# A spectral gate with a feed-forward layer on one Trainium2 core: the last six pairs of w1 columns in seven half-size products

## The chip, the core and the metric

The kernel runs on one core of a Trainium2 chip. A core has TensorE (matrix products, "PE" in the profile, its weight loads "PEld"), VectorE ("DVE"), ScalarE ("ACT"), GpSimd ("POOL") and SyncE ("SP", which here only issues transfers). Each engine works through its own queue in the order in which the kernel writes its instructions, and waits where data or a buffer is missing. SBUF is the working memory of 128 partitions, and PSUM is the small memory of eight banks into which TensorE writes. The metric is the device time of one execution in microseconds.

## What is computed

```python
x  = A_x                                   # [1, 2048, 1024]
xn = layernorm(x)                          # over the last axis
X  = rfft2(xn) * (w_r + 1j * w_i)          # filter, [2048, 513]
s  = irfft2(X)
h  = silu(xn @ w1)                         # w1: [1024, 3584]
g  = silu(h @ w2)                          # w2: [3584, 1024]
out = x + s * g
```

All large products are made to nearly float32 precision with float16 operands: each operand is split into a high and a low half, and three matmuls (high x high, high x low, low x high) stand for one.

## The kernel before

**Two stages.** The first stage is `xn @ w1`. w1 has 28 tiles of 128 columns, and the 2048 rows of xn stand in four groups of 512, c = 0 to 3. One block (`mm1(c, f)`, L413) is 24 matmuls of 512 columns: eight slices of the 1024-long sum times three. It ends in one PSUM bank of the pool `pf`, which has four. The function that it returns empties the bank one block later with a ScalarE activation (Silu, L429). There are 112 blocks. Two w1 tiles make a pair q (0 to 13), and two row groups make a half g (0 or 1). When the four blocks of a pair and a half are done, `hidden` (L435) forms sums and differences of the four results, splits them into halves (ScalarE L216, then VectorE L219), and stores them in DRAM. They are the left operands of the second stage.

**The second stage** is `h @ w2`, already in seven products of half size (Strassen's scheme), m = 0 to 6. `w2_gen` (L367) loads the blocks of w2, or sums of them prepared in DRAM, and splits them. `mm2` (L494) multiplies and `acc` (L515) adds up on VectorE. Of the seven weight operands, three are sums that `w2max_gen` (L327) makes on VectorE and stores while it looks for the largest value of w2. Two more are summed by accumulating transfers (`SUMMED`).

**Background work.** Layer norm and the Fourier work run in between. `ln_gen(c)` (L643) normalises group c: `stats` takes mean and variance, and for c = 2 and 3 (`TURNED`) `turned` (L614) normalises on ScalarE, splits, and lets transfers transpose the halves. `fd_gen(c)` (L743) is the transform along the columns, `f_gen` (L872) the transform along the rows and the filter in 16 units, and `i_gen(c)` (L1100) the inverse. `weights1` (L226) loads w1 tiles, takes their largest value for a scale, and splits them. `wmax_gen` (L839) takes the largest value of the filter in 18 tiles.

**The order of the work** is written out by hand at build time. After each block, `after` (L1268) writes the pending steps of earlier blocks (`settle`), and `work` (L1274) takes one step of the w1 or w2 queue, one step of the queue of maxima in three of four calls, and up to three steps of the background queue:

```python
clock["dve"] = max(clock["dve"], clock["pe"] - 1.0)
for _ in range(3):
    if clock["dve"] > clock["pe"] + LEAD or hold[0] or slot(bg) == PAUSE:
        break
```

The two clocks are the planner's own tally of what it has written for VectorE and TensorE (`meter`, L179). ScalarE, GpSimd and transfers have no clock. The loop over `order` (from L1320 on) writes all 112 blocks: groups 0 and 1 with six tiles first, then groups 2 and 3 with the same six, then the rest pair by pair. The queue of maxima starts at block 22, when layer norm is done. The background queue holds ln, the four `fd_gen`, the filter and the inverse, in this order.

Of the kernel before, what the change touches and what calls it, by code (L numbers as in the profile page):

```python
# [9 lines left out]
F16 = mybir.dt.float16  # L10
# [12 lines left out]
LEAD, PAUSE, LAST, EARLY = 1.0, -1, 6, 2  # L23
IORDER = (1, 3, 0, 2)
SUMMED = (4, 5)
# [7 lines left out]
W2_BLOCKS = (((0, 0), (1, 1)), ((1, 0), (1, 1)), ((0, 0), (0, 1)), ((0, 0),), ((1, 0), (0, 0)), ((0, 1), (1, 1)), ((1, 1),))  # L33
RH = math.sqrt(0.5)
# [3 lines left out]
def _halves(v, scale):  # L38
    v = v * scale
    hi = v.astype(np.float16)  # L40
    return hi, (v - hi.astype(np.float64)).astype(np.float16)

# [54 lines left out]
def spectral_ffn(ctx, tc, x, w_r, w_i, w1, w2, ca, kc, ci, tw, pm, out):  # L97
# [11 lines left out]
    fp = ctx.enter_context(tc.tile_pool(name="fp", bufs=1))  # L109
    hstack = ExitStack()  # L110
# [9 lines left out]
    ws = {m: [dp.tile([128, 512], F32, name=f"ws{m}_{q}") for q in range(NP)] for m in range(3)}  # L120
# [9 lines left out]
    xsv = cp.tile([128, 3, 4, 4, 2], F32, name="xsv")  # L130
    e_w = small("e_w")
# [78 lines left out]
    e1, m1, r1, rs, s1 = (small(k, NFT) for k in ("e1", "m1", "r1", "rs1", "s1"))  # L210
    ep, hs = small("ep", NP), small("hs", NP)
    w2m = small("w2m", NFT)
# [8 lines left out]
    def column_sums(name, m, n):  # L221
        ps = pf.tile([128, 512], F32, name=name, tag="ff")
        nc.tensor.matmul(ps[:, 0:n], ones, m, start=True, stop=True)
        return ps[:, 0:n]

    def weights1():  # L226

        raw = {}

        def load(i):
            raw[i] = fp.tile([128, 8, 128], F32, name=f"w1r{i}", tag="w1", bufs=7)
            nc.sync.dma_start(raw[i], w1v[:, :, i * 128:(i + 1) * 128])
# [4 lines left out]
        def scales(i, k):  # L241
            sl = slice(i, i + k)
            ps = column_sums(f"s1_{i}", m1[:, sl], k)
            nc.vector.tensor_single_scalar(e1[:, sl].bitcast(I32), ps.bitcast(I32), 0x7F800000, op=OP.bitwise_and)
            nc.vector.tensor_single_scalar(e1[:, sl], e1[:, sl], 2.0**-100, op=OP.max)
            nc.vector.reciprocal(r1[:, sl], e1[:, sl])
            nc.vector.tensor_single_scalar(rs[:, sl], r1[:, sl], 2.0**14, op=OP.mult)  # L247
            nc.vector.tensor_single_scalar(s1[:, sl], e1[:, sl], 2.0**-24, op=OP.mult)
            if (i + k) % 2 == 0:
                p = (i + k) // 2 - 1  # L250
                nc.vector.tensor_tensor(ep[:, p:p + 1], e1[:, 2 * p:2 * p + 1], e1[:, 2 * p + 1:2 * p + 2], op=OP.max)
                nc.vector.tensor_tensor(hs[:, p:p + 1], r1[:, 2 * p:2 * p + 1], r1[:, 2 * p + 1:2 * p + 2], op=OP.min)
                nc.vector.tensor_single_scalar(hs[:, p:p + 1], hs[:, p:p + 1], 2.0**7, op=OP.mult)

        new = {}

        def split(i):
            new[i] = fp.tile([128, 2, 8, 128], F16, name=f"w1_{i}", tag="w1", bufs=7)
            high(new[i][:, 0], raw[i], rs[:, i:i + 1])

        def rest(i):
            w1t[i] = w = new.pop(i)
            low(w[:, 1], raw.pop(i), rs[:, i:i + 1], w[:, 0])
# [8 lines left out]
        scales(0, 2)  # L272
# [9 lines left out]
        scales(2, 2)  # L282
# [5 lines left out]
        yield 2  # L288
        def ahead(i):

            if i < NFT and i not in raw and i - len(used1) <= 4:
                load(i)
                load(i + 1)

        last = None
        for i in range(4, NFT, 2):
# [6 lines left out]
            maxi(i)  # L303
            if last is not None:
                rest(last)
            yield 0
            maxi(i + 1)
            yield 0
            ahead(i + 2)
# [3 lines left out]
            scales(i, 2)  # L313
            yield 0.8
            split(i)
            ahead(i + 2)
            yield 0.2
            rest(i)
            split(i + 1)
# [3 lines left out]
        rest(last)  # L323

    used1 = set()

    def w2max_gen():  # L327

        ap = A["p"]
        junk = ap.tile([128, 1024], F16, name="junk", tag="junk", bufs=1)  # L330
        tiles = {}
        for i in range(NFT + 3):
            if i < NFT:
                tiles[i] = ap.tile([128, 1024], F32, name=f"w2m{i}", tag="x", bufs=4)
                nc.sync.dma_start(tiles[i], w2[i * 128:(i + 1) * 128, :])
            if 3 <= i <= NFT + 2:
                def both(m, x0, x1, op):
                    d = ap.tile([128, 512], F32, name=f"wd{m}_{i}", tag="wd", bufs=3)
                    nc.vector.tensor_tensor(d, x0, x1, op=op)
                    defer(1, lambda q=(i - 3) // 2: stores[0].dma_start(ws[m][q], d))  # L340

                t_ = tiles.pop(i - 3)
                if i % 2:
                    both(0, t_[:, 0:512], tiles[i - 2][:, 512:1024], OP.subtract)
                both(1 + i % 2, t_[:, 0:512], t_[:, 512:1024], OP.add)
                nc.scalar.activation(junk, t_, AF.Abs, accum_out=w2m[:, i - 3:i - 2])
# [6 lines left out]
    def w2_scales():  # L353
# [7 lines left out]
        nc.vector.tensor_scalar(c2, e2, ee, 2.0**-20, op0=OP.mult, op1=OP.mult)  # L361
# [4 lines left out]

    def w2_gen():  # L367

        todo = [(m, q) for m in range(7) for q in range(NP)]
        raw = {}  # L370
# [23 lines left out]
        for n in range(4):  # L394
            load(n)
# [1056 lines left out]
```

## Time and profile before

| | us |
|---|---|
| median of two runs | 1293.58 |
| the runs | 1291.99 and 1295.17 |
| span of the profiled execution | 1291.9 |
| TensorE busy in it | 1264.8 |
| VectorE busy in it | 958.6 |
| ScalarE busy in it | 463.9 |
| GpSimd busy in it | 242.3 |

The profiled execution's own time is its span. A row of the groups reads: line of the kernel, engine, operation, output <- inputs, partitions x elements, count, then busy us and mean ns of one, then the idle time of the engine just before these instructions and what ended most of it. In the order of time a row reads: start us, duration us, engine, line, operation, and in brackets the idle time before it and what ended it. The row of a wait reads: engine, operation and line that waited, what it waited for, us in all, times, longest. The row of a transfer reads: output <- input, queue, count, KB of one, median us from issue to landing. "issue" is time for which the profile shows no cause.

### The profile page before, as it was taken

What the parts mean: (1) busy time and instruction counts of PE and PEld (TensorE: products, weight loads), DVE (VectorE), ACT (ScalarE), POOL (GpSimd) and SP (SyncE); (2) the same over time, 40 slices, a digit from 0 to 9 for tenths busy, and PEclk for the clock granted to TensorE, in tenths of its full rate; (3) what the DMA queues carried; (4) which work ended last, traced back from release to release, by engine and by line L of the source; (5) the groups of instructions that cost most, each with busy time, mean ns of one, the idle gap of its engine ahead of it and who ended that gap; (6) DMA issues with size and microseconds to landing.
All of it is one profiled execution on the core that took longest, in us unless ns stands there. A gap on an engine that the chain in (4) does not pass through costs nothing.

```text
span 1291.9 us, 18825 instructions
## 1 busy us (share of the span) xinstructions
PE 1264.8 (98%) x6991; PEld 656.7 (51%) x6991; DVE 958.6 (74%) x1964; ACT 463.9 (36%) x572; POOL 242.3 (19%) x389
## 2 busy tenths in 40 slices
PE   8999999999999999999999999999979999999997
PEld 5544445444544454445455555554445555656444
DVE  6688898899879898867679798993165565867544
ACT  4864343343545565534242311220131321333111
POOL 1231222223233443241221010104110100000000
PEclk9998999999999999999999999999989999999999
DMA  7576476555766896579889999984996799675995
GB/s 232 132 188 178 123 227 191 164 149 181 230 194 236 278 296 205 190 230 269 179 252 259 270 278 199 336 213 146 305 259 229 218 323 339 241 285 167 313 360 187
DMA packets 174955, 298.84 MB, mean 231 GB/s; under 512 B 38928, under 2 KB 91920, under 8 KB 174224
## 3 DMA queue, kind: packets, MB, share of 16 engines
q1 hardware_dynamic: 132464, 163.34, 42.5%
q0 software_dynamic: 26560, 82.86, 21.3%
q10 hardware_dynamic: 15840, 51.45, 11.3%
q8 instruction: 55, 0.90, 0.3%
q14 instruction: 36, 0.29, 0.1%
HBM read 189.06 MB, written 104.33 MB: 227 GB/s over the span
## 4 chain that ended last, share of the span: by engine, by line
PE 82%; DMA 8%; DVE 5%; ACT 2%; issue 2%; POOL 1%; SPq 0%; ACTq 0%; DVEq 0%; POOLq 0%
PE pa L420 39%; PE pb L498 10%; PE pb L499 10%; PE pb L500 10%; PE iu L1117 3%; PE id L1146 3%; DMA jr<-ws 2%; DMA hd_one<-hoone 2%; PE fx L902 1%; DMA zt<-zd 1%; ACT xp L657 1%; DMA jr<-in_B_w_dram 1%; DVE w L219 1%; DMA ht<-hd_sum 1%; PE fx L904 1%
## 5 line engine op out<-in xcount | busy, mean ns | idle before, releaser
L420 PE MATMUL pa<-xnT,w 128*128 128x512 f16 x2688 | 587.7, 380 | 5.6 <-DMA xnT<-xs 3.2
L420 PEld LDWEIGHTS <-w 128*128 128x128 f16 x2688 | 263.2, 98 | 319.0 <-issue 8.3
L498 PE MATMUL pb<-w,ht 128*128 128x512 f16 (+1 forms) x798 | 299.5, 375 | 0.2 <-DMA ht<-hd_sum_d 0.2
L499 PE MATMUL pb<-w,ht 128*128 128x512 f16 (+1 forms) x798 | 299.5, 375 | 0.0
L500 PE MATMUL pb<-w,ht 128*128 128x512 f16 (+1 forms) x798 | 299.5, 375 | 0.0
L429 ACT ACTIVATE h<-pa,s 128x512 f32<-128x512 f32 x112 | 75.8, 680 | 142.5 <-PE pa L420 135.7
L500 PEld LDWEIGHTS <-ht 128*128 128x128 f16 x798 | 78.1, 98 | 91.1
L498 PEld LDWEIGHTS <-ht 128*128 128x128 f16 x798 | 78.2, 98 | 88.5 <-DMA ht<-hd_sum_d 0.7
L499 PEld LDWEIGHTS <-ht 128*128 128x128 f16 x798 | 78.1, 98 | 87.8
L216 ACT ACTIVATE w<-jr,sc 128x512 f16<-128x512 f32 x98 | 67.7, 713 | 85.3 <-DMA jr<-in_B_w_dram 39.8
L219 DVE SCALAR_TENSOR_TENSOR w<-jr,sc,w 128x512 f16<-128x512 f32 x98 | 72.1, 748 | 25.9 <-ACT w L216 25.8
L219 DVE SCALAR_TENSOR_TENSOR hoone<-h,hs,hoone 128x2048 f16<-128x2048 f32 x28 | 65.8, 2348 | 19.6 <-ACT hoone L216 19.6
L452 POOL DMA_DIRECT2D hd_sum<-hosum x52 | 38.0, 767 | 209.8 <-DVE hosum L219 101.7
L216 ACT ACTIVATE hoone<-h,hs 128x2048 f16<-128x2048 f32 x28 | 55.9, 1997 | 40.3 <-DMA hd_one<-hoone 27.9
L216 ACT ACTIVATE hosum<-hr,hs 128x1536 f16<-128x1536 f32 x28 | 44.1, 1574 | 59.4 <-DVE hr L459 32.1
L452 POOL DMA_DIRECT2D hd_one<-hoone x52 | 45.5, 875 | 86.5 <-DVE hoone L219 52.5
L380 POOL DMA_DIRECT2D jr<-in_B_w_dram x28 | 24.6, 966 | 165.0 <-DMA jr<-in_B_w_dram 129.6
L458 DVE TENSOR_TENSOR hr<-h 128x1024 f32<-128x1024 f32 x28 | 34.2, 1223 | 28.0 <-ACT h L429 27.8
L1117 PE MATMUL iu<-kk,zt 128*128 128x256 f16 x384 | 45.3, 280 | 8.7 <-issue 8.7
L219 DVE SCALAR_TENSOR_TENSOR hosum<-hr,hs,hosum 128x1536 f16<-128x1536 f32 x28 | 50.8, 1814 | 1.9 <-ACT hosum L216 1.9
L216 ACT ACTIVATE w<-w1r,rs 128x1024 f16<-128x1024 f32 x28 | 32.0, 1146 | 49.6 <-DVE rs L247 20.2
L579 ACT ACTIVATE pl<-pl,c 128x512 f32<-128x512 f32 (+1 forms) x26 | 16.9, 682 | 89.5 <-DVE pl L558 45.9
(195 smaller groups left out, 1686.0 us busy)
## 6 DMA issues: line engine op xcount, KB each, us to landing
w1r<-in_B_w_dram SPq DMA_DIRECT2D x28, 512.0 KB, 6.2
w2m<-in_B_w_dram SPq DMA_DIRECT2D x28, 512.0 KB, 5.0
ht<-hd_dif ACTq DMA_DIRECT2D x32, 448.0 KB, 7.9
jr<-in_B_w_dram SPq DMA_DIRECT2D x56, 256.0 KB, 7.3
ht<-hd_sum ACTq DMA_DIRECT2D x32, 448.0 KB, 6.2
ht<-hd_one ACTq DMA_DIRECT2D x32, 448.0 KB, 5.2
hd_sum<-hosum POOLq DMA_DIRECT2D x52, 256.0 KB, 3.4
hd_one<-hoone POOLq DMA_DIRECT2D x52, 256.0 KB, 5.1
```

The costliest lines, as they stand in the source:

```text
L216: nc.scalar.activation(hi, raw, AF.Copy, scale=scale)
L219: nc.vector.scalar_tensor_tensor(lo, raw, scale, hi, op0=OP.mult, op1=OP.subtract)
L380: nc.gpsimd.dma_start(raw[n], w2_block(*todo[n], 1), accum_op=OP.add)
L420: nc.tensor.matmul(ps, w[:, wh, d], xt[:, xh, d], start=(n == 0), stop=(n == 23))
L429: nc.scalar.activation(hq[:, 2 * (c % 2) + f % 2], ps, AF.Silu, scale=s1[:, f:f + 1])
L452: defer(1, lambda k=k, m=m: stores[0].dma_start(hd[m, g][:, :, q].rearrange("f p h s -> f p (h s)"), o[:, k].rearrange("f p h s -> f p (h ...
L458: tt(sums[:, 0:2], hq[:, 0::2], hq[:, 1::2], op=OP.subtract)
L498: nc.tensor.matmul(ps, hh[:, 0], w[:, 0], start=first, stop=False)
L499: nc.tensor.matmul(ps, hh[:, 0], w[:, 1], start=False, stop=False)
L500: nc.tensor.matmul(ps, hh[:, 1], w[:, 0], start=False, stop=last)
L1117: nc.tensor.matmul(ps[:, q], lhs, rhs, start=(n == 0 and r == 0), stop=(n == 2 and r == 1))
L1146: nc.tensor.matmul(o, us[g][:, uh, 2 * p + r], C["ci"][:, ch, g, r], start=(n == 0 and r == 0), stop=(n == 2 and r == 1))
```

## The change

**w1.** The first 16 tiles are multiplied as before (64 blocks). The last six pairs are multiplied in seven half-size products each, per half g of the rows: the 1024-long sum is cut in two, the pair into its two tiles, the half into its two groups. `product(q, g, name)` is 12 matmuls. The products M1, M6, M7 and M4 add up in one PSUM bank, M5 and M3 go on in a second, M2 has a bank of its own, and ScalarE copies the first bank's partial sum out between the products:

```diff
+SLOTS = (("M1", 0), ("M6", 2), ("M5", 3), ("M7", 4), ("M2", 5), ("M4", 6), ("M3", 8))
+    def product(q, g, name):
+        a_, b_, s_ = W[q]
+        x0, x1, t_ = xnT[2 * g], xnT[2 * g + 1], T[g]
...
+        if name == "M1":
+            ae = pt.tile([128, 2, 512], F32, name=f"ae{q}_{g}", tag="ft")
+            units[q, g] = [ae[:, 0], ae[:, 1], None]
+        if name == "M2":
+            units[q, g][2] = pf.tile([128, 512], F32, name=f"pc{q}_{g}", tag="ff")
+        a, e, f = units[q, g]
+        ps = {"M2": f, "M3": e, "M5": e}.get(name, a)
+        for d in range(4):
+            for n, (wh, xh) in enumerate(((0, 0), (0, 1), (1, 0))):
+                nc.tensor.matmul(ps, lhs(d, wh), rhs(d, xh), ...)
...
+            if name == "M1":
+                act(hq[:, 2], a, AF.Copy)
+            elif name == "M6":
+                act(hq[:, 0], a, AF.Copy)
+            elif name == "M7":
+                act(hq[:, 1], a, AF.Copy)
+                tt(hq[:, 1], hq[:, 1], e, op=OP.add)
+                return lambda: (act(hq[:, 1], hq[:, 1], AF.Silu, scale=sc), None)[1]
+            elif name == "M4":
+                act(hq[:, 3], a, AF.Silu, scale=sc)
+            elif name == "M2":
+                tt(hq[:, 2], hq[:, 2], f, op=OP.add)
...
+            elif name == "M3":
+                tt(hq[:, 0], hq[:, 0], e, op=OP.add)
```

A unit is one (q, g); its products take places 7n + the offset in `SLOTS`, so that neighbouring units overlap by one product. The activation waits a stage after each add, and `hidden` follows as before.

**Operands.** `t_gen(g)` makes the sums of x that four of the products need, on VectorE and ScalarE, in the background queue after the first two `fd_gen`. `weights1` makes, for each of the last pairs, the split first tile, half of the second, and the split sums:

```diff
+    def t_gen(g):
...
+        for d in range(4):
+            b = view(R2[0], at * KB, [128, 4, 512], F32)
+            tt(b[:, 0:2], x1[:, 0, d::4], x1[:, 1, d::4], op=OP.add)
+            tt(b[:, 2:4], x0[:, 0, d::4], x0[:, 1, d::4], op=OP.add)
+            tt(b[:, 0], b[:, 2], b[:, 0], op=OP.subtract)
...
+            nc.scalar.activation(t_[:, d, :, 0], b, AF.Copy)
+            tt(t_[:, d, :, 1], b, t_[:, d, :, 0], op=OP.subtract)
+        for q in range(NPL, NP):
+            while not built[0]:
+                yield 0
+            r = view(R2[0], 64 * KB, [128, 2, 8, 128], F32)
...
+            high(a[:, 0], r[:, 0], sc)
+            low(a[:, 1], r[:, 0], sc, a[:, 0])
...
+            tt(r1[1], r1[0], r1[1], op=OP.add)
+            tt(r1[0], r0[0], r1[0], op=OP.subtract)
+            tt(r0[0], r1[1], r0[0], op=OP.subtract)
+            tt(r0[1], r0[1], r0[0], op=OP.subtract)
+            high(s_[:, 0, 0:8], rf[:, 0:8], sc)
```

`built` is true once the sums of x are done, and the first product comes only then.

**Memory.** xn, the sums of x and the weights stand in three fixed regions (`X1`, `R2`, `R3`), of which later tiles are views. `R2` opens only when the tiles of the first stage's pool are given back: `narrow` sets `hold_x`, which stops new loads in the queue of maxima, waits until the loaded tiles are used, and closes the pool. `hold_x` falls when the loop over the 64 blocks is done.

**Order.** The queue of maxima now takes w2 first (five steps for each two tiles), then the filter. What is left of it when the last pair starts is written out at once:

```diff
-LEAD, PAUSE, LAST, EARLY = 1.0, -1, 6, 2
+LEAD, PAUSE, EARLY = 2.5, -1, 2
+    for n, (_, u, name) in enumerate(plan):
...
+        if not w2j and (w1j.done and not xq or q == NP - 1):
+            finish(wq, w1j)
+            while xq:
+                slot(xq)
+            w2_scales()
+            w2j = add(wq, w2_gen())
+        ev = product(q, g, name)
```

The transforms of groups 2 and 3, and the whole filter, come in the second stage, and in the inverse some pauses go.

**Who does what.** The statistics of groups 2 and 3, and most maxima of w1, move to ScalarE:

```diff
+            if c in TURNED:
...
+                nc.scalar.activation(junk, xt, AF.Copy, accum_out=v[:, 0:1])
+                nc.gpsimd.tensor_single_scalar(v[:, 0:1], v[:, 0:1], -1.0 / D, op=OP.mult)
+                nc.scalar.activation(junk, xt, AF.Square, bias=v[:, 0:1], accum_out=v[:, 3:4])
...
+    def magnitude(raw, out):
+        junk = pf.tile([128, 512], F32, name="junk", tag="ff")
+        for k in range(2):
+            nc.scalar.activation(junk, raw[:, 512 * k:512 * k + 512], AF.Abs, accum_out=out[:, k:k + 1])
```

`magnitude` takes the sum of absolute values in place of the largest one. Two of the three sums of w2 that VectorE made are now made by accumulating transfers (`SUMMED = (1, 2, 4, 5)`). The column transform does two row tiles in one instruction, and in the filter a reordering moves from the butterflies to the split that follows them, so that both take fewer VectorE instructions. A pair of w1 tiles shares one scale.

673 lines of the change are left out of this document (443 added, 230 removed).

## The prediction

> **What bounds the kernel now.** I read the page first: engine sums, the TensorE clock by slices, the chain that ended last.
>
> ```profile
> span 1291.9 us, 18825 instructions
> PE 1264.8 (98%) x6991; PEld 656.7 (51%) x6991; DVE 958.6 (74%) x1964; ACT 463.9 (36%) x572; POOL 242.3 (19%) x389
> PEclk9998999999999999999999999999989999999999
> PE 82%; DMA 8%; DVE 5%; ACT 2%; issue 2%; POOL 1%; SPq 0%; ACTq 0%; DVEq 0%; POOLq 0%
> ```
>
> TensorE is busy 1264.8 of 1291.9 us, at full clock in nearly every slice, and is 82% of the chain. So the time is TensorE's work plus its few waits, and a change pays only if TensorE is still fed. Next I read the groups of instructions and busy times by stretch (after the colon of each stretch: its length, then PE, PEld, DVE, ACT, POOL busy, granted clock, DMA share, GB/s).
>
> ```profile
> L420 PE MATMUL pa<-xnT,w 128*128 128x512 f16 x2688 | 587.7, 380 | 5.6 <-DMA xnT<-xs 3.2 <-DVE xnT L674 1.7 <-ACT w L216 0.7
> 0.00:646.00 646.00, 635.28 (x3350) 312.61 (x3351) 531.27 (x1048) 308.09 (x346) 187.47 (x286) 0.99 0.68 204
> 646.00:1292.00 646.00, 629.52 (x3643) 344.14 (x3641) 427.36 (x916) 155.85 (x226) 54.79 (x103) 0.99 0.83 259
> 576.00:878.00 302.00, 300.90 (x1773) 156.93 (x1771) 253.83 (x489) 88.25 (x118) 40.34 (x64) 1.00 0.90 249
> ```
>
> The first product, 2688 matmuls at L420, fills the first 646 us and waits 5.6 us in all. VectorE is at 82% there (531 of 646), 66% in the second half, 84% in the stretch where the filter runs (576 to 878). None of that stops TensorE. What makes this work is slack: a block of 24 matmuls ends in one ScalarE activation, and four PSUM buffers let it come up to three blocks late. I therefore look at where the change spends that slack.
>
> **What it saves.** Blocks run back to back like this:
>
> ```profile
> 60.97 41.60 PE L420 MATMUL pa<-xnT,w 128*128 128x512 f16 x192
> 106.34 0.44 PE L420 MATMUL pa<-xnT,w 128*128 128x512 f16 x1 [2.43 <-DMA xnT<-xs]
> ```
>
> 192 matmuls in 41.60 us, the last one's run-out taken off, is 0.216 us each and 5.18 us a block. Seven products of 12 matmuls replace four blocks of 24, so 84 stand for 96. Six pairs times two groups are 12 units: 144 matmuls, **31.1 us** less. Other TensorE work only moves: two of four column transforms and all filter matmuls go to the second half. TensorE there has the same total, so I count the move at nothing; its cover is VectorE's free time, and the third rival prices its loss.
>
> **Layer norm on ScalarE, the start.** For column groups 2 and 3 the statistics go from VectorE to two ScalarE passes a tile. The planner hands out up to three background steps a block, while its VectorE clock is no more than LEAD ahead of TensorE's. A step that costs VectorE nothing always passes, so the steps of groups 2 and 3, spread now over blocks 4 to 11, all come out behind blocks 4 and 5. ScalarE, in order, then has them ahead of those blocks' own activations. Its present order:
>
> ```profile
> 51.64 0.69 ACT L429 ACTIVATE h<-pa,s 128x512 f32<-128x512 f32 x1
> 58.54 0.67 ACT L429 ACTIVATE h<-pa,s 128x512 f32<-128x512 f32 x1
> 65.39 0.67 ACT L429 ACTIVATE h<-pa,s 128x512 f32<-128x512 f32 x1
> 65.95 1.14 ACT L216 ACTIVATE w<-w1r,rs 128x1024 f16<-128x1024 f32 x1
> 71.42 1.15 ACT L216 ACTIVATE w<-w1r,rs 128x1024 f16<-128x1024 f32 x1 [4.33 <-DVE w L219]
> ```
> ```profile
> L657 ACT ACTIVATE xp<-x,v 128x1024 f32<-128x1024 f32 x8 | 17.3, 2163 | 0.0
> L635 ACT ACTIVATE xs<-xp 128x1024 f16<-128x1024 f32 x8 | 8.5, 1057 | 0.3
> L346 ACT ACTIVATE junk<-w2m 128x1024 f16<-128x1024 f32 x28 | 29.3, 1045 | 0.0
> L346 ACT ACTIVATION_READ_ACCUMULATOR junk<-w2m 128x1 f32 x28 | 5.3, 190 | 0.0
> ```
>
> These are the activations of blocks 3, 4 and 5, then the splits of the fifth and sixth w1 tiles. Normalising and splitting two tiles is 2 x (2.16 + 1.06) = 6.4 us. A statistics pass with its sum is 1.05 + 0.19 (the row nearest in form), so 4.9 us for two tiles. The activation of block 3 slides by 4.9 to 56.6. Ahead of block 4's then stand one w1 maximum (two 512-wide passes by the 0.69 row with their sums, 1.7), 6.4, 4.9 and 6.4: it starts at 56.6 + 0.7 + 19.4 = 76.7 instead of 58.5. Ahead of block 5's stand 4.9 + 6.4 + 4.9 + 6.4 = 22.6: it starts at 100.0. The fifth tile's split comes after that. With 1.14 and VectorE's low half (1.28, below) the tile is there at about 103, and block 8, which multiplies by it, began at 60.97 + 2 x 5.18 = 71.3. That is 32 us late, less the transposes' wait at 106 that falls away, plus slow clock:
>
> ```profile
> 104.00:108.00 4.00, 0.93 (x3) 0.31 (x4) 3.90 (x14) 3.89 (x4) 0.00 (x0) 0.81 0.91 186
> 108.00:112.00 4.00, 4.00 (x11) 1.44 (x10) 4.00 (x17) 0.00 (x0) 1.91 (x3) 0.50 0.38 116
> 112.00:116.00 4.00, 4.00 (x17) 1.63 (x15) 3.90 (x7) 0.45 (x1) 2.22 (x4) 0.83 0.67 196
> ```
>
> Here a wait of 3.1 us (4.00 - 0.93) was followed by 4 us at half clock and 4 at 0.83: 2.7 us lost beside the wait. Two new waits cost 5, the old one gives back 6. I take **+30**. Bounds: 15, if the new ScalarE work alone counts and fills the 4.3 us gap of the last row (8 tiles x 2.5 = 20, less that), and 45, if the loads for group 3, which now queue on SP behind all transposes of group 2, hold it as well.
>
> [...]
>
> **The hand-over to the seven products.** Its sums of x are the last background work before it. Prices:
>
> ```profile
> L219 DVE SCALAR_TENSOR_TENSOR hoone<-h,hs,hoone 128x2048 f16<-128x2048 f32 x28 | 65.8, 2348 | 19.6 <-ACT hoone L216 19.6
> L219 DVE SCALAR_TENSOR_TENSOR hosum<-hr,hs,hosum 128x1536 f16<-128x1536 f32 x28 | 50.8, 1814 | 1.9 <-ACT hosum L216 1.9
> L219 DVE SCALAR_TENSOR_TENSOR w<-w1r,rs,w 128x1024 f16<-128x1024 f32 x28 | 35.8, 1278 | 2.4 <-ACT w L216 2.4
> L458 DVE TENSOR_TENSOR hr<-h 128x1024 f32<-128x1024 f32 x28 | 34.2, 1223 | 28.0 <-ACT h L429 27.8
> L459 DVE TENSOR_TENSOR hr<-h 128x512 f32<-128x512 f32 x28 | 19.2, 686 | 0.0
> L239 DVE TENSOR_REDUCE m<-w1r 128x1 f32<-128x1024 f32 x28 | 33.9, 1214 | 5.5 <-DMA w1r<-in_B_w_dram 5.5
> L850 DVE TENSOR_REDUCE mw<-wm 128x1 f32<-128x912 f32 x18 | 19.7, 1096 | 0.0
> w1r<-in_B_w_dram SPq DMA_DIRECT2D x28, 512.0 KB, 6.2
> wm<-in_A_w_r_dram SPq DMA_DIRECT2D x9, 456.0 KB, 3.9
> wm<-in_A_w_i_dram SPq DMA_DIRECT2D x9, 456.0 KB, 3.7
> ```
>
> Eight rounds of 2 x 1.22 + 4 x 0.69 + 2.35 are 60 us. Beside them VectorE has per block a quarter of the hidden tiles' work (1.22 + 0.69 + 1.81 + 1.22 + 2.35 = 7.3) and some 0.35 of w1, 2.2 of 5.18 us, so the sums need about 20 blocks. They begin when the two transforms are done and the held queue of w2 maxima has drained. That queue starts at block 22, moves one step in three of four blocks and needs five steps for each of the three pairs that it holds by then: 15 steps, block 42 to 44 of 64. So the sums end with the last block. Only then may the first pair be loaded, into a place that the sums used. Two loads (6.2 each, overlapped, some 8), a maximum (1.2), a scale (1), high and low (1.14 + 1.28) are 12.6, less the 5.2 of the last block; M6 then waits some 3.5 more for the sums of the weights. **+11**; nothing if the sums end ten blocks earlier, 20 if VectorE runs behind.
>
> **In the products.** Five results of a unit share one bank: ScalarE must copy the partial sum before the next product adds, with one product (2.6 us) between. I take **+4**: 36 copies hidden cost 0, exposed 36 x 0.69 = 25; ScalarE is 48% busy in the first stage, so nearer the low end. VectorE's added work (60 for x, 36 adds of 0.69, four adds and one and a half lows more a pair) is some 113 us. It gives up 12 maxima of w1, 28 sums of w2 and eight tiles' statistics, 14.6 + 19.2 + 12 (the statistics as two 512-wide passes each, by L459): some 1026 us in all beside 1261 of time, so by its total it holds nothing up.
>
> **The burst before the last pair.** Maxima of w2 and of the filter advance one step in three of four products and stand still from the hold to the hand-over. 70 products give 52 steps; eleven of 14 pairs of w2 tiles are left at five steps each, so all 18 filter tiles remain, and the code drains them at once when the last pair starts. VectorE then takes 18 x 1.10 = 19.7 us without anything between, or, with three buffers of 3.8 to land and 1.1 to read, 18 x 1.63 + 3.8 = 33. Behind it in VectorE's queue is the low half of the hidden tile two units back, whose buffer M1's copy needs; M6 adds to what that copy reads. So TensorE gets two products (5.2 us), then waits: 19.7 + 2.4 + 0.7 - 5.2 = 17.6 up to 31. **+26**, nearer the loads' bound, slow clock within.
>
> **The second half.** More background work falls into it: two transforms and the first filter units. Its cover is the 34% of VectorE that is free there (646 - 427 = 219 us). The wait of TensorE in it today,
>
> ```profile
> PE iu L1117 <- issue: 8.7, 1, 8.7
> ```
>
> may come or go. Taken at **0**, between -9 and the +25 of the third rival.
>
> Sum on the profiled 1291.9: -31 + 30 + 11 + 4 + 26 = +40, **1332**; the median of the runs shown is 1.7 above the span, so **1334**.
>
> **Rivals.** *TensorE stays fed* (faster): ScalarE has 52% free in stage one, the pairs come in time, the drain hides behind PSUM buffers. For it: TensorE waits for ScalarE 0.7 us in all today. Against: those buffers do not cover a chain within one bank, nor 20 us of one queue. Time 1293.6 - 31 = 1262, or 1257 without the wait at 106; it decides if the new waits together stay under 5 us. Chance 0.18. *Half of it* (the same): the start or the drain is absorbed, not both: 1334 - 28 = 1306, or 1280 with the hand-over too. 0.2. *The late stage binds*: column transforms, filter and inverse in one half put VectorE, at 84% in 576 to 878 over 302 us, on the same filter in some 225 us, with DMA already 0.90; or every copy in the bank is exposed. 20 to 25 more: 1357. 0.1. The forecast has the remaining 0.52. That nothing is saved cannot be: the count of matmuls is fixed.
>
> **The numbers.** Two per cent, about what a measurement here can tell from no change, is 1267.7 and 1319.5. The forecast's own range is 1312 to 1352, from the bounds of the two largest terms half used up. The whole range, 1270 to 1362, leaves out most of the first rival and the worst of the third. Faster is the first rival, 0.18; within 2% the second and the low edge of the forecast, 0.25; slower 0.57.
>
> **What would show it.** TensorE idle 66 to 105 us with ScalarE solid in norms; a gap of some 10 us where the first block of 12 starts; a gap of about 25 before the last pair with 18 reductions in a row on VectorE; 2544 matmuls in place of 2688. If ScalarE's activations of blocks 4 and 5 start within 15 us of their blocks' ends, the first term is wrong; if the filter's reductions lie spread, the fourth is.

## The result, and the profile after

The changed kernel takes 1467.92 us (two runs, 1467.06 and 1468.78) against 1293.58: 1.135 times as long, with a 95% interval of 1.131 to 1.140. The prediction was 1334, with a range of 1270 to 1362. It was right that the kernel gets slower; the time lies 106 us above the top of the range.

The page of the changed kernel, in the lines that were shown of before:

```profile
span 1465.3 us, 18532 instructions
PE 1263.1 (86%) x6851; PEld 653.4 (45%) x6851; DVE 1002.4 (68%) x1696; ACT 570.6 (39%) x828; POOL 279.6 (19%) x417
PEclk9958999999979999985989999999898899989999
PE 25%; DMA 14%; DVE 9%; issue 2%; ACT 1%; POOL 1%; SPq 1%; ACTq 0%; DVEq 0%; POOLq 0%
```

TensorE is busy as long as before (1263.1 against 1264.8) with 140 fewer instructions. The chain that ended last is followed back only to about 686 us here, so its shares add up to 53% of the span; TensorE is 25 of these 53, where it was 82 of 100. The clock digits (TensorE's granted clock in tenths of full speed, in 40 slices) show where the time went: slices 3 and 4 (the start), 12 (the hand-over), 18 and 19 (before the last pair), and single ones in the second half. Cut at the first matmul of the second product, after and then before:

```profile
0.00:727.50 727.50, 599.33 (x2904) 281.21 (x2905) 492.66 (x650) 375.54 (x511) 173.46 (x276) 0.93 0.52 156
727.50:1465.30 737.80, 663.80 (x3949) 372.16 (x3947) 509.77 (x1047) 195.07 (x317) 106.09 (x141) 0.95 0.85 255
```
```profile
0.00:644.70 644.70, 633.98 (x3344) 312.02 (x3345) 531.27 (x1048) 308.09 (x346) 187.47 (x286) 0.99 0.68 203
644.70:1291.90 647.20, 630.82 (x3649) 344.73 (x3647) 427.36 (x916) 155.85 (x226) 54.79 (x103) 0.99 0.83 259
```

Length less PE busy is TensorE's idle time. In the first stage it goes from 10.7 to 128.2 us (+117.5), in the second from 16.4 to 74.0 (+57.6). So the whole loss, 173.4 in the spans, is 175.1 of idle time less 1.7 of busy time. Busy time falls by 34.7 in the first stage and rises by 33.0 in the second. The work that moved is smaller than that: half of the column transforms' 23.55 us and 8.28 us of the filter stood in the first stage before, 20.1 in all. So the second stage is busy 12.9 us longer than the moved work explains, and the first stage falls by 34.7 where the move and the 31.1 us saved would make 51.2. Together that is 29.4 us: nearly all that the fewer matmuls save goes in slower matmuls, at a granted clock of 0.93 and 0.95 (0.99 before).

What TensorE waited for, the largest lines of the view of waits:

```profile
PE ae L605 <- ACT h L617: 43.3, 6, 35.9
PE pa L565 <- ACT w L264: 35.8, 2, 35.3
PE iu L1377 <- DVE xn L1367: 31.4, 3, 12.6
PE fx L1124 <- DMA xn<-vd: 14.6, 3, 11.9
PE ae L605 <- ACT h L625: 12.6, 5, 9.5
PE s L279 <- DVE m L392: 10.8, 3, 8.2
PE fa L944 <- DMA r<-in_B_w_dram: 10.4, 1, 10.4
PE ae L605 <- ACT h L619: 8.2, 12, 0.7
```

L565 is a block of the first product as before, L605 one of the half-size products, fa, fx and iu are matmuls of the transform, the filter and the inverse. The names xn, r and w are now those of the three fixed regions, whatever stands in them.

**The start** went as the prediction says. ScalarE in the order of time, and the stretch of TensorE (of after, then of before):

```profile
55.00 0.71 ACT L575 ACTIVATE h<-pa,ep 128x512 f32<-128x512 f32 x1
...
74.91 0.67 ACT L575 ACTIVATE h<-pa,ep 128x512 f32<-128x512 f32 x1
82.36 1.06 ACT L854 ACTIVATE junk<-x 128x1024 f16<-128x1024 f32 x1 [6.77 <-DMA x<-in_A_x_dram]
...
106.07 0.67 ACT L575 ACTIVATE h<-pa,ep 128x512 f32<-128x512 f32 x1
106.64 1.14 ACT L264 ACTIVATE w<-w,rs 128x1024 f16<-128x1024 f32 x1
```
```profile
66.00:113.00 47.00, 8.40 (x53) 4.04 (x52) 11.90 (x16) 33.40 (x36) 7.26 (x24) 0.61 0.46 109
```
```profile
66.00:113.00 47.00, 43.83 (x208) 19.83 (x207) 40.45 (x61) 29.66 (x25) 12.38 (x15) 0.93 0.78 189
```

L575 are the activations of blocks 3, 4 and 5; between them stand two groups of statistics and norms. In 47 us TensorE does 53 instructions where it did 208.

**Before the last pair**, TensorE and then VectorE:

```profile
648.06 5.27 PE L605 MATMUL ae<-xn,w 128*128 128x512 f16 x12 [9.53 <-ACT h L625]
689.18 7.78 PE L605 MATMUL ae<-r,w 128*128 128x512 f16 x24 [35.86 <-ACT h L617]
```
```profile
647.59 1.09 DVE L1072 TENSOR_REDUCE mw<-xn 128x1 f32<-128x912 f32 x1
653.33 1.10 DVE L1072 TENSOR_REDUCE mw<-r 128x1 f32<-128x912 f32 x1 [4.64 <-DMA r<-in_A_w_i_dram]
...
682.25 1.10 DVE L1072 TENSOR_REDUCE mw<-xn 128x1 f32<-128x912 f32 x1
686.10 2.34 DVE L267 SCALAR_TENSOR_TENSOR hoone<-h,hs,hoone 128x2048 f16<-128x2048 f32 x1
```

The 18 reductions are in a row, most of them waiting for a load; behind them comes the low half of the hidden tile (hoone), and behind that the copy (L617) for which TensorE waits.

### The profile page after: what moved, and what is told of

It reads as the page before. It is cut to its first block, busy times and chain, and to the rows that moved or that the text cites. A ratio compares the mean times of both kernels' runs of the same rounds, so it can differ in the third digit from the quotient of the medians.

```text
span 1465.3 us, 18532 instructions
## 1 busy us (share of the span) xinstructions
PE 1263.1 (86%) x6851; PEld 653.4 (45%) x6851; DVE 1002.4 (68%) x1696; ACT 570.6 (39%) x828; POOL 279.6 (19%) x417
## 4 chain that ended last, share of the span: by engine, by line
PE 25%; DMA 14%; DVE 9%; issue 2%; ACT 1%; POOL 1%; SPq 1%; ACTq 0%; DVEq 0%; POOLq 0%
PE pb L700 6%; PE pb L701 6%; PE pb L702 6%; PE iu L1377 3%; DMA r<-in_B_w_dram 3%; DMA xn<-vd 2%; DMA zd<-xn 2%; PE id L1406 2%; PE ae L605 2%; DMA xn<-zd 2%; DMA fs<-gd 1%; DVE r L267 1%; DMA pd<-c 1%; PE fx L1124 1%; DMA xn<-in_A_w_i_dram 1%
## 5 line engine op out<-in xcount | busy, mean ns | idle before, releaser
L565 PE MATMUL pa<-xn,w 128*128 128x512 f16 x1536 | 336.6, 381 | 41.6 <-ACT w L264 35.8
L700 PE MATMUL pb<-r,w 128*128 128x512 f16 (+1 forms) x798 | 299.8, 376 | 0.0
L701 PE MATMUL pb<-r,w 128*128 128x512 f16 (+1 forms) x798 | 299.6, 375 | 0.0
L702 PE MATMUL pb<-r,w 128*128 128x512 f16 (+1 forms) x798 | 299.5, 375 | 0.0
L565 PEld LDWEIGHTS <-w 128*128 128x128 f16 x1536 | 150.3, 98 | 224.4 <-ACT w L264 36.3
L605 PEld LDWEIGHTS <-w 128*128 128x128 f16 x1008 | 100.5, 100 | 199.3 <-issue 82.8
L605 PE MATMUL ae<-r,w 128*128 128x512 f16 x576 | 135.2, 389 | 55.2 <-ACT h L617 43.3
L702 PEld LDWEIGHTS <-w 128*128 128x128 f16 x798 | 78.1, 98 | 91.4 <-issue 0.5
L700 PEld LDWEIGHTS <-w 128*128 128x128 f16 x798 | 78.3, 98 | 87.2 <-issue 0.2
L701 PEld LDWEIGHTS <-w 128*128 128x128 f16 x798 | 78.2, 98 | 87.1
L264 ACT ACTIVATE r<-r,sc 128x512 f16<-128x512 f32 x88 | 61.6, 716 | 130.2 <-DMA r<-in_B_w_dram 108.5
L267 DVE SCALAR_TENSOR_TENSOR r<-r,sc 128x512 f16<-128x512 f32 x88 | 65.0, 746 | 40.7 <-ACT r L264 40.7
L605 PE MATMUL ae<-xn,w 128*128 128x512 f16 x288 | 69.2, 395 | 14.7 <-ACT h L625 12.6
L1377 PE MATMUL iu<-xn 128*128 128x256 f16 x384 | 48.8, 293 | 31.4 <-DVE xn L1367 31.4
L505 POOL DMA_DIRECT2D r<-in_B_w_dram x56 | 49.8, 1042 | 136.3 <-DMA r<-in_B_w_dram 135.2
L1124 PE MATMUL fx<-xn 128*128 128x256 f16 x192 | 50.5, 301 | 25.9 <-DMA xn<-vd 14.6
```

The lines of the kernel that those rows point to most:

```text
L264: nc.scalar.activation(hi, raw, AF.Copy, scale=scale)
L267: nc.vector.scalar_tensor_tensor(lo, raw, scale, hi, op0=OP.mult, op1=OP.subtract)
L505: nc.gpsimd.dma_start(raw[n], w2_block(m, q, 1), accum_op=OP.add)
L565: nc.tensor.matmul(ps, w[:, wh, d], xt[:, xh, d], start=(n == 0), stop=(n == 23))
L605: nc.tensor.matmul(ps, lhs(d, wh), rhs(d, xh), start=(name in ("M1", "M2", "M5") and d + n == 0), stop=(d + n == 5), skip_group_check=True)
L700: nc.tensor.matmul(ps, hh[:, 0], w[:, 0], start=first, stop=False)
```

## The experiments

The theory after this reading: four separate losses, at the start (ScalarE's statistics), at the hand-over (the sums of x end too late), in the products (the queue of maxima), and in the second stage (matmuls written right behind what they need, or VectorE, or transfers). Each kernel below was run once; the kernel before, run beside it, took 1292.45 to 1293.21 us. A difference of 4 us or less is taken for none.

### Statistics back on VectorE

```diff
-            if c in TURNED:
+            if False:
```

> The changed kernel, with the layer-norm statistics of row groups 2 and 3 back on VectorE. Theory (ScalarE, loaded with two groups of norms at once, makes the wait at the start): TensorE's 35.3 us wait for the split of the fifth w1 tile goes, with the 3.3 us behind it and some 5 us of slow clock; a wait of 3 to 6 us for the transposes may come back. 1468 - 38 = about 1430. Rival (the two groups' norms in one burst would hold ScalarE anyhow, statistics or not): of ScalarE's chain only the 8 x 2.5 = 20 us of statistics go, so 15 to 20 us come off: about 1450.

Measured: 1438.32, 29.6 less. The wait of 35.3 is gone; TensorE still waits 5.8 us there (4.1 for a low half, 1.7 for a split), and 4.7 for the activation of a block later, at 166 us. In size the result lies between the two: the statistics decide whether the 35 us wait is there, and some of it comes back in small ones.

### The same part alone, in the kernel before

The same eight statistics were put on ScalarE in the kernel before, with nothing else of the change.

> The kernel before with one part of the change: the layer-norm statistics of row groups 2 and 3 in two passes on ScalarE. Theory (that part alone holds ScalarE with two groups of norms, so the fifth w1 tile's split comes late): TensorE waits for that split around 70 to 105 us, 20 to 35 us in all: 1293 + 25 = about 1318. Rival (it takes ScalarE's maxima of w1 as well, which only the change has there, or the statistics ride in ScalarE's free time): 1290 to 1300.

Measured: 1307.23, 14.0 more, between the two forecasts. The mechanism shows, in TensorE's waits between 60 and 110 us:

```profile
PE pa L420 <- DVE w L219: 9.5, 2, 9.1
PE pa L420 <- ACT h L429: 8.1, 1, 8.1
PE pa L420 <- ACT w L216: 3.9, 1, 3.9
```

These are 21.5 us, less the old wait for transposes, which falls away. The 14.0 are about half the price that the statistics have in the changed kernel. Two things differ there: the maxima of w1 stand in ScalarE's queue as well, and the planner's lead is 2.5 in place of 1.0. Between 50 and 125 us TensorE is busy 71.8 us in the kernel before, 53.5 in this one, 48.0 in the changed kernel with LEAD at 1.0 (below) and 35.8 with 2.5. By these numbers more of the difference goes with the lead than with the maxima; neither was tried alone in the kernel before.

### No drain before the last pair

```diff
             after(ev)
+            slot(xq)
```

> The changed kernel with one more step of the queue of maxima after each of the 84 half-size products, so that nothing is left to be drained before the last pair. Theory (the drain makes the 9.5 and 35.9 us waits): both go, with some 6 us of slow clock: 1468 - 50 = about 1418. Rival (the work only moves: VectorE, which then has the 18 reductions of 1.1 us among the products, makes TensorE wait there): less than 20 us come off, about 1450, with waits of TensorE spread over the products.

Measured: 1455.45, only 12.5 less: the rival. The waits of 35.9 and 9.5 are gone, and others stand in their place; but VectorE's load is not what makes them. One, on ScalarE (first two rows) and TensorE:

```profile
485.55 0.60 ACT L285 ACTIVATE junk<-xn 128x512 f32<-128x512 f32 x1 [8.14 <-DMA xn<-in_B_w_dram]
...
486.93 0.58 ACT L617 ACTIVATE h<-ae 128x512 f32<-128x512 f32 x1
```
```profile
487.56 7.90 PE L605 MATMUL ae<-r,w 128*128 128x512 f16 x24 [9.32 <-ACT h L617]
```

ScalarE stands at the maximum of a w2 tile (L285) that is not loaded yet, and the copy of the partial sum comes right behind that maximum in its queue. The load had waited for its place and was issued at 480.96: the difference of w2 is now made in the tile itself and stored from there, and in the changed kernel SyncE waits for such stores ahead of the loads of w2 (L442), us in all, times, longest:

```profile
SPq L442 <- DMA ws<-xn: 106.6, 7, 20.0
```

With three places the queue of maxima runs at the pace of load, difference and store.

### Maxima after, and maxima before the sums

The first kernel starts the whole queue of maxima at the first half-size product; the second takes all of w2 before the sums, while the pool still has four buffers.

```diff
-                max_job = add(xq, w2max_gen())
-                add(xq, wmax_gen())
...
         hold_x[0] = False
+        add(xq, w2max_gen())
+        add(xq, wmax_gen())
```
```diff
-        hold_x[0] = True
-        while live_x[0]:
+        while not max_job.done:
             yield PAUSE
...
             after(ev)
+            if t_job:
+                for _ in range(3):
+                    slot(xq)
```

> As the run with spread maxima, and the whole queue of maxima starts only at the first half-size product, so that the sums of x need not wait for it. Theory (the sums end with block 64 because the queue of maxima is emptied three pairs deep at three steps in four blocks): the sums end some ten blocks or more earlier, the first pair is loaded and split in time, and the 8.2 + 3.5 us waits and the holes at the hand-over (15.6 us in all, with some 4 us of slow clock) go: 15 to 20 us under the run with spread maxima alone, about 1400. Rival (VectorE itself is what makes the sums late): the hand-over keeps its gap, and 0 to 5 us come off; with 10 more tiles' maxima of w2 in the products (16 us of ScalarE), the time could also grow by up to 10.

> The changed kernel with all 28 maxima of w2 and their 14 differences taken before the sums of x, at some four steps a block from block 22 on, where the pool still has four buffers; the filter's 18 maxima follow among the products at up to two steps a product. Theory (with three places left, each freed only when the difference made in it has been stored, the queue of maxima runs at the pace of load, difference, store, and ScalarE and VectorE, in order, hold the copies of the partial sums behind it): the waits in the products (some 80 us of TensorE idle and slow clock between 424 and 727 us) fall to about 25, and these 303 us to some 245; the first 64 blocks may wait for ScalarE, up to 15 us: about 1420. Rival (VectorE's and ScalarE's own work in the products makes the waits): the stretch of the products keeps 285 us or more, and the time stays over 1450.

Measured: 1461.06 for the first, 5.6 more than with the drain spread, where the theory had 15 to 20 less and the rival up to 10 more; 1428.08 for the second, 39.8 less than the changed kernel. The first kernel settles the hand-over. TensorE from 395 to 425 us, with the maxima late and then in the changed kernel:

```profile
395.00:425.00 30.00, 30.00 (x141) 13.58 (x140) 13.70 (x13) 11.30 (x12) 8.00 (x11) 1.00 0.40 115
```
```profile
395.00:425.00 30.00, 18.97 (x87) 8.83 (x85) 21.17 (x22) 11.23 (x10) 7.41 (x11) 0.88 0.44 132
```

Without the queue of maxima in their way the sums are done in time and the gap is gone. But then every tile of w2 goes through the three places among the products, and more is lost there. The second kernel bears out the theory of the products: from the first to the end they take 260 us in place of 303, and the largest waits left in them are these:

```profile
PE ae L605 <- DVE h L622: 11.2, 3, 5.7
PE ae L605 <- ACT h L619: 8.2, 12, 0.7
PE ae L605 <- ACT h L617: 7.9, 6, 2.6
```

This kernel takes ScalarE's own work on w2 out of the products as well, some 29 us of it (busy 150.9 us from the first product to 730 in the changed kernel, 121.7 here), so the time alone does not part that work from the chain of loads and stores. The rows at 485 us above do: there the copy stands behind a step that waits 8.14 us for its load.

### Both fixes

> The statistics back on VectorE and the maxima of w2 taken before the sums, both in one kernel. Theory (the wait at the start and the waits in the products are two independent losses): the gains add up, 29.6 + 39.9: 1468 - 69 = about 1398. Rival (the time won at the start is lost again where the earlier maxima load ScalarE in the first 64 blocks): 1410 to 1425.

Measured: 1398.64, 69.3 less. The sum of the two single gains is 69.4: the start and the products are independent losses.

### Empty steps in the second stage

```diff
         open_fd()
-        yield PAUSE
+        for _ in range(4):
+            yield PAUSE
...
+        for _ in range(3):
+            yield PAUSE
         load_k(0)
...
         nc.vector.tensor_copy(zt[:, :, :, :, 0, 0], zp[:, c])
+        for _ in range(3):
+            yield PAUSE
```

> The changed kernel with empty planner steps in the second stage alone: three between the load of the transform's constants and the third column transform, five more around the filter's first loads, two more ahead of and three behind the small copy that opens each inverse transform. Theory (the second stage waits where a load or a short VectorE step is written just ahead of the matmuls that need it): the waits of 10.4, 11.9 and 31.4 us go, some 54 us with slow clock, and the second stage falls from 738 to about 690: 1468 - 48 = about 1420. Rival (transfers, 0.94 busy from 885 to 1130 us, or VectorE bind the second stage): the waits come out elsewhere in it, and it stays at 725 to 740.

Measured: 1540.39, 72.5 more; neither forecast had that. The transforms end too late. The last of the four inverses, TensorE in the order of time, first in the changed kernel (its last matmuls only), then with the empty steps, rows left out at the dots:

```profile
1392.61 2.78 PE L1406 MATMUL id<-xn 128*128 128x256 f16 x24
```
```profile
1462.49 9.31 PE L1382 MATMUL iu<-xn 128*128 128x256 f16 x72 [24.40 <-DVE xn L1370]
...
1486.95 6.63 PE L1411 MATMUL id<-xn 128*128 128x256 f16 x50 [0.22 <-DVE xn L1401]
```

In the changed kernel this inverse ends at 1395, 70 us ahead of the end of the span, with products beside it. Here it runs after all products but the last, with no other matmul in its waits. With two transforms and the filter in it, the second stage's background chain, from 727 to the last of its matmuls at 1395, takes 668 of the stage's 738 us. (The 118 us that a later expectation names is the distance from the end of the third inverse, at 1347.)

### LEAD back at 1.0, and up to 4.0

> The changed kernel with LEAD back at 1.0. Theory (in the second stage VectorE's queue is written too far ahead, so short steps that TensorE needs stand behind up to 2.5 us of planned work and whatever waits in it): the waits for the copy ahead of the inverse (31.4 us) and for the filter's butterflies (11.3) shrink by half, some 20 us with slow clock: about 1445. Rival (VectorE's backlog comes from VectorE waiting for transfers, not from the planner's lead): 0 to 5 us, 1463 to 1475, with the background work a few blocks later.

Measured: 1543.54, 75.6 more; neither had that either. TensorE waits 38.4 us for the maximum of the first pair at the hand-over (until 439.73), since the sums end later still, and the last inverse, 1467 to 1509, again runs after the products. The longer lead, which the prediction only named in passing, is worth more than the saving of the products. More of it is worth nothing, by the last run:

> The kernel with all working edits (1388) and LEAD 4.0 in place of 2.5. Theory (the background's chain is as long as the stage, and the planner's lead limits how early it runs; from 1.0 to 2.5 the lead won 75 us): the sums and the inverse come earlier, 0 to 12 us less, 1376 to 1388. Rival (2.5 is enough, and a longer lead only puts more work ahead of what TensorE needs at once): 1390 to 1410.

Measured: 1391.24, against 1387.92 with 2.5: 3.3 more, taken for none.

### Three small edits

```diff
-        nc.vector.tensor_copy(zt[:, :, :, :, 0, 0], zp[:, c])
+        nc.gpsimd.tensor_copy(zt[:, :, :, :, 0, 0], zp[:, c])
...
             ev = product(q, g, name)
+            if name == "M6":
+                ev()
+                ev = lambda: None
```

Besides, there are two more empty steps between the filter's first loads and its first matmuls.

> Three small edits of the changed kernel, each with a wait of its own to show it. The 16-element copy that opens each inverse goes from VectorE to GpSimd: if VectorE's backlog in front of it makes the 31.4 us wait, that falls under 5; if the load that it reads is late, it stays. Two more empty steps between the filter's first loads and its first matmuls: the wait for that load falls from 11.9 to under 4. The copy of the partial sum after M6 is written ahead of M5 in place of behind it: if it waits for M5 only because M5 was written first, the 12 waits of 0.69 us (8.2 in all) go; if any two uses of the two-bank tile are kept apart, they stay, as waits of M5. All three: 1468 - 45 = about 1423. Rival (nothing is won because the second stage is bound by VectorE or by transfers behind these waits): 1455 or more.

Measured: 1458.75, 9.2 less. The waits at the inverse fall only from 31.4 to 25.6. 13.3 of these are the first inverse, on TensorE and GpSimd:

```profile
1178.47 10.52 PE L1377 MATMUL iu<-xn 128*128 128x256 f16 x72 [13.28 <-POOL xn L1367]
```
```profile
1178.16 0.26 POOL L1367 COPY xn<-zp 128x16 f16<-128x16 f16 x1 [20.98 <-DMA xn<-zd]
```

So there it is the load that is late, as the expectation allowed. At the later inverses the copy has left VectorE's backlog, and TensorE waits 12.3 us further on, for a VectorE step that reads its PSUM results (L1387). The filter's wait stays (14.6 and 15.5). The copy after M6 gives a plain answer. In the changed kernel, TensorE:

```profile
516.55 5.34 PE L605 MATMUL ae<-r,w 128*128 128x512 f16 x24 [0.97 <-ACT h L617]
522.58 2.75 PE L605 MATMUL ae<-r,w 128*128 128x512 f16 x12 [0.69 <-ACT h L619]
```

M6 and M5 run together, and M7 waits 0.69 for a copy that starts only when M5 ends. With the copy written ahead of M5:

```profile
515.21 2.75 PE L605 MATMUL ae<-r,w 128*128 128x512 f16 x12 [0.97 <-ACT h L617]
518.64 5.34 PE L605 MATMUL ae<-r,w 128*128 128x512 f16 x24 [0.69 <-ACT h L619]
```

Now M6 is alone, and M5 waits the same 0.69. The two banks are one tile, and in both kernels the use of it that is written second waits for the first, 0.69 us in each of 12 units, 8.2 in all.

### Six empty steps, and all working edits together

> The changed kernel with six empty planner steps in the second stage in place of the 26 of the earlier run: one between the copy that opens an inverse and its matmuls (four times), two ahead of the filter's first matmuls. Theory (these matmuls are written right behind what they need, and the background's chain ends 118 us ahead of the end, so there is room for a few steps, 4.5 us each, but not for 26): the 31.4 us at the inverses fall to some 15, the 14.6 at the filter to some 5, with slow clock some 30 us: about 1440. Rival (VectorE is behind by more than one step at each inverse, and every empty step costs the chain as much as it saves): 1460 to 1480.

Measured: 1455.49, 12.4 less. The waits at the inverse fall to 22.1, those at the filter grow to 16.9. Between theory and rival: the empty steps help, but less than was hoped.

> All the edits that are free of the 26 empty steps, together: statistics on VectorE, maxima of w2 before the sums, the small copy of the inverse on GpSimd with one empty step behind it, two before the filter. Theory (three losses, each with its own cause): 1398 less 20 to 30 in the second stage, about 1370, which leaves some 75 us over the kernel before: the second stage's own waits, the copies in the bank, and what is left of the start. Rival (the second stage has no room): 1395 or more.

Measured: 1387.92, 10.7 under both fixes, in place of 20 to 30, and between theory and rival. This is the best version found, 80 us under the changed kernel and 95 over the one before.

### VectorE or the transfers, in the second stage

Two runs leave out accumulating transfers of w2 (the 28 that the change added, then all 56), one some of VectorE's work in the filter, one both.

```diff
-            if m in SUMMED:
+            if m in SUMMED[2:]:
```
```diff
-            if m in SUMMED:
+            if m in ():
```
```diff
-            tt(t2, Xv, wi.unsqueeze(2).broadcast_to([128, 4, 2, 128]), op=OP.mult)
+            t2 = t1
...
-            tt(b2, Y[:, 0:2], Y[:, 2:4], op=OP.add)
-            tt(d2, Y[:, 0:2], Y[:, 2:4], op=OP.subtract)
+            b2, d2 = Y[:, 0:2], Y[:, 2:4]
```

> The changed kernel without the 28 accumulating transfers that the change added (the second halves of two of the seven operands of w2 are left out). Theory (at the start of the second stage transfers are at their limit, 1.00 to 1.07 busy from 735 to 765 us, and the constants of the third transform, issued at 754.6, land late): 28 x 256 KB, some 7.3 MB of about 190 MB, go, TensorE's 10.4 us wait at 765 falls under 4, and the second stage shortens by 10 to 20 us: about 1452. Rival (the wait is one of order on the queue that issues, behind loads that wait for a place): the wait at 765 stays at 8 to 11 and the time within 5 us of 1468.

> The changed kernel with less VectorE work in the filter: one of its two products (1.2 us) and the two butterflies behind (0.7 each) are left out in each of 16 units, 42 us in all, and nothing else. Theory (VectorE's own work binds the second stage): the filter's stretch, 245 us from 885 to 1130, shortens by TensorE's waits in it, and the backlog at the inverse falls: 20 to 35 us less, about 1440. Rival (late operands of w2 hold ScalarE, and VectorE behind it): under 8 us, 1460 or more.

> The changed kernel without any accumulating transfer of w2 (the second halves of four of the seven operands are left out, 56 transfers of 256 KB in place of the 28 of the earlier run). Rival (late operands of w2 hold ScalarE, and VectorE and TensorE behind it): ScalarE's 108 us of waits for them fall under 40, as before the change, and the time falls by 15 to 30: about 1445. Theory (VectorE's work binds): ScalarE waits less, but the time falls by 8 at most, 1460 or more.

> Both parts left out, of the filter and of the sums of w2. If one of the two binds alone, this is within 5 us of the better of the two runs; if each hides the other, it is 20 us or more under both.

Measured: 1464.88 without the 28 added transfers, 1459.16 with the lighter filter, 1438.83 without any of the 56, 1436.82 with both left out. VectorE's own work is not the main limit: 35.7 us less of it (1002.4 to 966.7 busy; 42 was expected) bring 8.8, and 2.0 where the transfers are left out too. Leaving out all 56 transfers brings 29.1, about a third of the 90.6 us by which the second stage grew. ScalarE's waits for the operands of w2, before the change (two rows), in the changed kernel, without 28 and without 56:

```profile
ACT w L216 <- DMA jr<-in_B_w_dram: 39.8, 12, 7.5
ACT w L216 <- DMA jr<-ws: 13.8, 2, 11.2
```
```profile
ACT r L264 <- DMA r<-in_B_w_dram: 108.5, 32, 11.6
```
```profile
ACT r L264 <- DMA r<-in_B_w_dram: 88.6, 21, 12.3
```
```profile
ACT r L264 <- DMA r<-in_B_w_dram: 18.5, 6, 7.4
```

An operand that is summed by a transfer is loaded, then GpSimd waits for that load and issues the second (135.2 us of GpSimd's waits in the changed kernel, in 28 of them, 13.0 at most), and only then ScalarE may split it; behind ScalarE's split stand VectorE's low half and the rest of both queues. Leaving out the added 28 alone won 3.0 us, no more than the runs tell from nothing, although TensorE's wait of 10.4 at 765 us went; the wait for the filter's loads grew from 14.6 to 22.9. By subtraction most of the 29.1 goes with the 28 transfers that were there before. Whether they cost as much in the old second stage was not tried, so it is not shown that the change made them dear.

## Why the prediction missed by 134 us

In the spans the miss is 133.4 us. With the 20.1 us of moved work taken from the first stage and added to the second, the prediction had the first stage grow by 19.9 and the second by 20.1. They grew by 82.8 and 90.6, so 62.9 of the miss lie in the first stage and 70.5 in the second.

*The saving, 31 us.* The count of matmuls was right: 2544. The time was not won: the waits of 9.53 and 35.86 us were each followed by 4 us at a granted clock of 0.50 (648 to 652 and 689 to 693), and busy time fell by 1.7 in all.

*The start, +30.* Right, step by step: block 4's activation was forecast for 76.7 and came at 74.91, block 5's for 100.0 and came at 106.07, with 6.77 us of waiting for a load of x, which the upper bound had named. TensorE's idle time ahead of the blocks of the first product rose from 5.6 to 41.6. Shown by taking the statistics back: 29.6.

*The hand-over, +11.* Right in mechanism and near in size: 8.18 + 1.03 + 1.82 + 0.29 and then 3.53 for M6 are 14.9 us idle, and slow clock comes on top (0.88 from 395 to 425 us, 0.71 from 425 to 430). Shown by the late maxima.

*Copies in the bank, +4.* Mis-sized. It measured 18.9: 8.2 at M7, 7.4 and 3.1 in the other rows of waits for ScalarE once the two long ones are taken off, 3.7 for VectorE, less the 3.5 of M6 at the hand-over, which is in the 7.4. I took the low end of 0 to 25 because ScalarE was 48% busy. The share did not tell; what stands ahead of the copy in the queue did, and 8.2 of it was the two banks kept apart as one tile. (Four products add up in the bank, not five; the 36 copies are right.)

*The burst, +26.* Mis-sized. The gap is where the forecast put it, with the 18 reductions and the low half behind them, but it is 9.53 + 35.86 = 45.4 us idle. Slow clock adds some 2.5 us behind each of the two waits: 12 matmuls took 5.27 us and 24 took 7.78, where the rows above have 2.75 and 5.34. The reductions came every 2.04 us (17 steps from 647.59 to 682.25), not every 1.63. The loads landed in 3.9 to 4.8 us (medians), not in 3.8, and the 9.53 is a wait for the last tiles of w2 ahead of the filter's; small scale steps of 2.7 us followed, which I had left out.

*The queue of maxima, priced as a drain alone.* This is the step behind the burst that failed. I gave the queue a price only for what is left at the end, and took from VectorE's total, 1026 of 1261 us, that among the products "it holds nothing up". The runs show that it costs wherever it stands among the products: with the drain spread over them, only 12.5 us came off, because copies that TensorE needs then stand behind its loads. Its pace is that of a chain of load, difference and store over three places, not that of VectorE's work. With the w2 part taken before the sums, the products took 43 us less and the kernel 39.8.

*The second half, 0.* This is the step that failed outright: 57.6 us of idle time and 12.9 of slower matmuls. I named "the 34% of VectorE that is free there" as its cover. VectorE had room, and taking work from it won 8.8. What was missing was time in the chain of dependent steps, which fills 668 of the stage's 738 us: 26 empty steps made the kernel 72.5 us longer, and with a shorter lead this stage took 64 us more (739.8 to 1541.8). Of the 70.5 us, 29.1 come off without the accumulating transfers of w2; that these cost more than before because the queues have no slack left is argued, not shown, and the cause of the rest stays open. The third rival, *the late stage binds*, was right in place and named VectorE first, with the DMA share of 0.90 beside it; it gave 20 to 25 more and a chance of 0.1.

*The other rivals.* Neither start nor drain was absorbed; both of the lower rivals needed at least one of them to be. (The second rival's 1280 does not follow from its terms either: 1306 less 11 is 1295.)

Not settled: where the 95 us of the best version come from one by one. Its second stage still takes 724 us, with 662 of TensorE's work.

## What to carry to other kernels

Count what stands in front of a short step in an in-order queue, not how busy the engine is: in the run without the drain a copy of 0.58 us stood behind a step that waited 8.14 us for its load, and TensorE waited 9.32 for the copy. When work is moved into another stage, check its chain of load, split, matmul and store against the length of that stage, not its busy time against an engine's free time (here the chain took 668 of 738 us, and VectorE was busy 510 of the 738). And if tiles are made fewer to win memory for an algorithm with fewer products, price the queue that used them at the pace of its loads and stores (SyncE waited 106.6 us, in 7 waits, for such stores in the changed kernel).

## What the hardware showed besides

After the wait of 35.86 us, 24 matmuls took 7.78 us where 24 take 5.34 behind a wait of 0.97: 2.4 us of slow clock. In windows of 4 us the granted clock was 0.50, 0.86 and 1.00:

```profile
689.00:693.00 4.00, 3.82 (x10) 1.33 (x10) 0.79 (x2) 0.74 (x2) 2.95 (x4) 0.50 0.80 239
693.00:697.00 4.00, 3.96 (x16) 1.59 (x15) 0.00 (x0) 0.00 (x0) 0.00 (x0) 0.86 0.41 153
697.00:701.00 4.00, 3.35 (x16) 1.55 (x16) 2.49 (x3) 2.99 (x6) 0.00 (x0) 1.00 0.00 0
```

The short waits of this kernel cost only themselves: from 440 to 640 us TensorE was idle 20.2 us in pieces of at most 1.57, and the granted clock was 1.00.
